# Pooled attention and a spatial gating unit on one core: the engines' order from a list schedule of the kernel's own, normalised rows on ScalarE, first operands early

## The chip, the core and the metric

The kernel runs on one core of one Trainium2 chip. The core has a matrix engine (TensorE, PE in the profile, with its weight loads as PEld), VectorE (DVE), ScalarE (ACT), GpSimd (POOL) and SyncE (SP), which here issues the DMA transfers. Each engine works through its own instructions in order; an instruction that depends on another engine's result waits for a semaphore. SBUF is the on-chip working memory, PSUM the memory of eight banks into which PE writes its products. The metric is the time of one execution in microseconds (us) of device time; the median of the runs is compared.

## The reference

`q`, `k` and `v` have 8 batches, 8 heads, 1152 rows and 64 columns. Attention runs with queries averaged in twos (576 per head); its output, with the heads side by side, goes through a gated unit whose second half is normalised by rows and mixed along the sequence.

```python
q_pool = q.reshape(B, H, S // 2, 2, D).mean(axis=3)
scores = scale * np.matmul(q_pool, k.transpose(0, 1, 3, 2))
attn = np.exp(scores - np.max(scores, axis=-1, keepdims=True))
x = attn / (attn.sum(-1) + 1e-9) @ v             # then heads beside each other: (8, 576, 512)
h = np.maximum(x @ w_in, 0.0)                    # w_in: 512 x 1024
u, v = h[..., :512], h[..., 512:]
v_n = (v - mean(v)) / np.sqrt(var(v) + 1e-6)     # per row
v_s = np.einsum('ts,bsd->btd', w_spatial, v_n) + b_spatial[None, :, None]
out = (u * v_s) @ w_out                          # w_out: 512 x 512
```

## The kernel before

**Pairs.** The 64 heads are worked on as 32 pairs (two heads of one batch; four pairs make a batch). A pair's work:

- `load_kq` and `load_v` (L230, L239) fetch keys, queries and values, 576 KB each.
- `prep` (L286) scales queries and keys by a power of two found from their squares (`square_sum` on ACT, a small matmul in `scales` L117) and splits each number into two 16-bit parts: `head` on ACT (L141), `rest` on DVE (L144), for the keys a subtraction on POOL (L319). Eleven or so DMAs on SP (L310 to L328) copy the parts to where both heads need them.
- `maxima` (L332) has PE form the scores once in one 16-bit product per tile, 27 tiles of 128 x 384 (L355, L346), and DVE take the row maximum of each (L361). `shift` (L369) turns the maxima into two rows of the operand `X`, so that the second pass subtracts them.
- `attention` (L520) forms the scores again, two matmuls a tile (L528, L529), and ACT takes the exponential into `pt` (L534): 18 main tiles of 512 columns. Columns 512 to 576 of both heads are the tail, `ptl` (L542). POOL splits the result into two 16-bit parts, two tiles at a time (L546).
- `values` (L435) multiplies by V (L449, L453, L458), accumulating in the PSUM bank `o`; `tail_values` (L492) does this for the tail (L500 to L502) in the columns of the same bank that the main part leaves free, without the check of accumulation groups. DVE divides by the row sums (L428, L429, L466, L506); `turn_main` (L473) transposes on PE and splits into `xg` (L422, L423).
- `norm_v` (L251) squares V for the scale of a batch, which needs all four pairs of it; `split_v` (L266) scales and splits V (L274, L275 on ACT, L277 on POOL).

**Units.** Two batches (8 pairs) make one of four units (`gated_unit`, L568): the v half of the hidden layer (L605, ReLU on ACT L613, row statistics on DVE L615, L616), a Newton iteration for the inverse root of the variances (L625 to L637, on DVE, all nine row tiles at once), the u half (L669, L679) with `normalise` (L639) once after each of the first nine pieces, the spatial product (L710, L711, L717, L720), a split of the gated result (`split`, L725) and the output product (L753, L773, L795). `normalise` is, per row tile, a subtract and multiply on DVE (L641), a cast to 16 bits on ACT (L646), the remainder on DVE (L647), and for one tile four copies.

The three weight matrices are also split into parts on the chip; `w_in` and `w_out` come as doubles, in pieces of 1024 KB (L187), and are taken apart on DVE and ACT (`from_double`, L150).

**What sets the order.** The program's order comes from the loop at L831: each step of a pair's attention lets the generators for the next pair's maxima, V, preparation and the weights go on at set rates, and `MOE_RATE` steps of a unit. The tile framework then puts the instructions of each engine in an order by its own scheduler and its own estimates, with program order as priority. Ahead of the loop (L819 to L827) stand the first pair's loads, its V squares, its preparation, the next pair's loads, V squares of the rest of the batch, the maxima and V's split.

**PSUM.** Eight banks: `ps_s` 3 (scores), `ps_m` 2 (maxima, small products, transposes), `ps_o` 1 (`o`), `ps_w` 2 (units; maxima too while no unit is under way, L341).

Of the kernel before, what the change touches and what calls it, by code (L numbers as in the profile page):

```python
# [10 lines left out]
F16 = mybir.dt.float16  # L11
BF16 = mybir.dt.bfloat16
F32 = mybir.dt.float32
I32 = mybir.dt.int32
I64 = mybir.dt.int64
U32 = mybir.dt.uint32
AF = mybir.ActivationFunctionType
ALU = mybir.AluOpType
AX = mybir.AxisListType
PSUM = bass.MemoryType.PSUM  # L20
# [8 lines left out]
PEXP = 2.0 ** 6  # L29


@with_exitstack
def attn_sgu_kernel(ctx: ExitStack, tc: tile.TileContext, qT, kT, v, w_in, w_spT, b_sp, w_out, out):
    nc = tc.nc
    P = 128
    B, NHP, _, D, _, S = qT.shape
    NC = kT.shape[4]
# [10 lines left out]
    NT = S2 // P  # L48
# [6 lines left out]
    D1 = D + 1  # L55
    VW = 2 * D + 2

    const = ctx.enter_context(tc.tile_pool(name="const", bufs=1))
    ld = ctx.enter_context(tc.tile_pool(name="ld", bufs=1))
    pp = ctx.enter_context(tc.tile_pool(name="pp", bufs=4))  # L60
    pt_ = ctx.enter_context(tc.tile_pool(name="pt_", bufs=1))
    wk = ctx.enter_context(tc.tile_pool(name="wk", bufs=2))
    mo = ctx.enter_context(tc.tile_pool(name="mo", bufs=1))
    sm = ctx.enter_context(tc.tile_pool(name="sm", bufs=1))
    ps_s = ctx.enter_context(tc.tile_pool(name="ps_s", bufs=3, space=PSUM))
    ps_m = ctx.enter_context(tc.tile_pool(name="ps_m", bufs=2, space=PSUM))
    ps_o = ctx.enter_context(tc.tile_pool(name="ps_o", bufs=1, space=PSUM))
    ps_w = ctx.enter_context(tc.tile_pool(name="ps_w", bufs=2, space=PSUM))


    nc.scalar.preload_act_table_set("natural_log_exp_and_others")
# [59 lines left out]
    def scale_of(sq, name):  # L131
        tot = sm.tile([P, 1], F32, name=name + "t", bufs=2)
        nc.vector.reduce_sum(out=tot, in_=sq, axis=AX.X)
        yield
        return (yield from scales(tot, name))

    def square_sum(acc, src, junk):
        nc.scalar.activation(junk, src, AF.Square, bias=0.0, scale=1.0, accum_out=acc)
# [89 lines left out]
    state = {}  # L228
# [10 lines left out]
    def load_v(i):  # L239
        b, hp = divmod(i, NHP)  # L240
        vt = ld.tile([P, 2, NC, D], F32, name="vt", bufs=2)
        nc.sync.dma_start(
            out=vt.rearrange("p h c d -> p h (c d)"),
            in_=v[b, 2 * hp : 2 * hp + 2].rearrange("h (p c) d -> p h (c d)", c=NC),
        )
        return vt
# [4 lines left out]
    def norm_v(i):  # L251

        b, hp = divmod(i, NHP)
        if hp == 0:
            vsq[b] = sm.tile([P, 2 * NHP], F32, name="vsq", bufs=2)
        vt = load_v(i)
        yield
        yield
        for h in range(2):
            square_sum(vsq[b][:, 2 * hp + h : 2 * hp + h + 1], vt[:, h], vt[:, h])  # L260
            yield
        if hp == NHP - 1:
            vscale[b] = yield from scale_of(vsq.pop(b), "v")
            yield
# [67 lines left out]
    def maxima(i):  # L332
        st = state[i]
        qhl, khh, X = st["qhl"], st["khh"], st["X"]
        W = KEYS // 3
        NB = W // P
        mt = sm.tile([P, NT, 3], F32, name="mt", bufs=2)
        for t in range(NT):
            for n in range(3):

                if units or (t + n) % 2:  # L341
                    pm = ps_m.tile([P, 512], F32, name="pm")
                else:
                    pm = ps_w.tile([P, 512], F32, name="pw")
                if t == 4:
                    nc.tensor.matmul(  # L346
                        pm[:, :W],
                        lhsT=qd[i % 2].rearrange("p h s -> p (h s)"),
                        rhs=st["kn"][:, n * NB : (n + 1) * NB, :],
                        start=True, stop=True,  # L350
                    )
                else:
                    h = 0 if t < 4 else 1
                    c0 = t * P if t < 4 else TAIL + (t - 5) * P
                    nc.tensor.matmul(  # L355
                        pm[:, :W],
                        lhsT=qhl[:, h, c0 : c0 + P],
                        rhs=khh[:, h, n * NB : (n + 1) * NB, :],
                        start=True, stop=True,
                    )  # L360
                nc.vector.reduce_max(out=mt[:, t, n : n + 1], in_=pm[:, :W], axis=AX.X)  # L361
                yield

            if t == 4 and True:
                yield from shift(X, mt, 0, 5)
        yield
        yield from shift(X, mt, 5 if True else 0, NT)
# [40 lines left out]
    xs = {}  # L408
# [83 lines left out]
    def tail_values(i):  # L492

        b, hp = divmod(i, NHP)
        ptl, vp = state[i]["ptl"], vps[i % 2]
        o = state[i]["o"][:, 4 * D1 : 6 * D1].rearrange("p (h d) -> p h d", d=D1)
        for c in range(NC):
            top = ptl.bitcast(BF16)[:, c].rearrange("p h s -> p (h s)")[:, 1::2]
            rst = ptl.bitcast(F16)[:, c].rearrange("p h s -> p (h s)")[:, 0::2]
            nc.tensor.matmul(o, lhsT=top, rhs=vp[:, :, c, D : D + D1], start=False, stop=False, skip_group_check=True)  # L500
            nc.tensor.matmul(o[:, :, 0:D], lhsT=top, rhs=vp[:, :, c, 0:D], start=False, stop=False, skip_group_check=True)
            nc.tensor.matmul(o, lhsT=rst, rhs=vp[:, :, c, D : D + D1], start=False, stop=c == NC - 1, skip_group_check=True)  # L502
        r = inverse(o[:, 0, D : D + 1], "dent")
        for h in range(2):
            rows = slice(h * D, (h + 1) * D)
            nc.vector.tensor_scalar_mul(xt[rows, hp, rows], o[rows, h, 0:D], r[rows])  # L506
# [61 lines left out]
    def gated_unit(un):  # L568
        b0, b1 = 2 * un, 2 * un + 1
# [5 lines left out]
        last = un == NU - 1  # L575
# [20 lines left out]
        vv = mo.tile([P, NT, DH], F32, name="vv")  # L596
        vh = vv.bitcast(F16)
        te = mo.tile([P, 2, DH], F16, name="te")
        mv = mo.tile([P, NT, 2], F32, name="mv")
        for t, (c0, _) in enumerate(tiles):  # L600
            ph = bank()
            n = 0
            for cc in range(NCC):
                for xa, wa in ((xh, wi_h), (xh, wi_l), (xl, wi_h)):
                    nc.tensor.matmul(  # L605
                        ph, lhsT=xa[:, cc, c0 : c0 + P], rhs=wa[:, cc, DH:DF],
                        start=n == 0, stop=n == 3 * NCC - 1,
# [4 lines left out]
            k = 0 if t < 4 else 2 if t == 4 else 1  # L612
# [11 lines left out]
        rs = sm.tile([P, NT], F32, name="rs")  # L624
        nc.vector.tensor_scalar_add(va, mv[:, :, 1], 1e-6)  # L625
        nc.vector.tensor_scalar(
            out=sd.bitcast(I32), in0=va.bitcast(I32), scalar1=1, scalar2=None, op0=ALU.logical_shift_right
        )
        nc.vector.tensor_scalar(
            out=rs.bitcast(I32), in0=sd.bitcast(I32), scalar1=-1.0, scalar2=float(0x5F3759DF), op0=ALU.mult, op1=ALU.add  # L630
        )
        for k in range(4):
# [3 lines left out]
            nc.vector.tensor_scalar(out=sd, in0=sd, scalar1=-0.5 * z, scalar2=1.5 * z, op0=ALU.mult, op1=ALU.add)  # L636
            nc.vector.tensor_mul(rs, rs, sd)  # L637

        def normalise(t):  # L639
            vn = wk.tile([P, DH], F32, name="row")  # L640
            nc.vector.tensor_scalar(  # L641
                out=vn, in0=vv[:, t, :], scalar1=mv[:, t, 0:1], scalar2=rs[:, t : t + 1],
                op0=ALU.subtract, op1=ALU.mult,
            )
            h, l = vh[:, t, 0:DH], vh[:, t, DH : 2 * DH]
            nc.scalar.activation(h, vn, AF.Copy, bias=0.0, scale=1.0)  # L646
            nc.vector.tensor_sub(l, vn, h)  # L647
            if t == 4:

                nc.vector.tensor_copy(out=te[0:TAIL, 0, :], in_=h[0:TAIL])  # L650
                nc.vector.tensor_copy(out=te[TAIL:P, 0, :], in_=l[0:TAIL])
                nc.vector.tensor_copy(out=te[0:TAIL, 1, :], in_=h[TAIL:P])
                nc.vector.tensor_copy(out=te[TAIL:P, 1, :], in_=l[TAIL:P])
# [9 lines left out]
        for fc in range(NFC):  # L663
            for a, z in pieces:
                pu = bank()
                n = 0
                for cc in range(NCC):
                    for xa, wa in ((xh, wi_h), (xl, wi_h), (xh, wi_l)):
                        nc.tensor.matmul(  # L669
                            pu[:, : z - a], lhsT=wa[:, cc, fc * P : (fc + 1) * P], rhs=xa[:, cc, a:z],  # L670
                            start=n == 0, stop=n == 3 * NCC - 1,
# [4 lines left out]
                for e in range(2):  # L676
                    y, w = max(a, e * S), min(z, (e + 1) * S)
# [87 lines left out]
        if not last:  # L765
# [4 lines left out]
            for t in range(NT):  # L770
                py = yield from products(0, t)
                y = wk.tile([P, DM], F32, name="row")
# [3 lines left out]
        else:  # L776
            order = [(e, fc) for fc in range(NFC) for e in range(2)]
# [14 lines left out]
            for t in range(NT):  # L792
                py = yield from products(1, t)
                y = vv[:, t]
# [20 lines left out]
    def drain(gen):  # L815
        while gen is not None:
            gen = step(gen)

    load_kq(0)  # L819
    drain(norm_v(0))  # L820
    drain(prep(0))
    load_kq(1)
    for i in range(1, NHP):
        drain(norm_v(i))
    drain(maxima(0))
    drain(split_v(0))
    drain(prep(1))  # L827
    weights = load_weights()
# [2 lines left out]
    for i in range(NP):  # L831
        if i + 2 < NP:
            load_kq(i + 2)
        run = [
            Pace(maxima(i + 1), MAX_RATE) if i + 1 < NP else None,
            Pace(values_ahead(i), V_RATE),
            Pace(prep(i + 2), PREP_RATE, PREP_AT) if i + 2 < NP else None,
            Pace(weights, W_RATE, W_AT if i == 0 else 0),
        ]
# [17 lines left out]
        turn(last=True)  # L857
    for g in units:
        drain(g)


def _lay(inputs):
# [42 lines left out]
```

## Time and profile before

| | |
|---|---|
| median of 3 runs | 1302.94 us (1302.19 to 1303.21) |
| profiled execution | 1300.77 us, span 1299.0 us |
| mean granted PE clock | 0.986 |
| busy: PE, ACT, DVE, POOL | 1175.9, 974.8, 894.7, 853.8 us |
| PE instructions | 13632 matmuls |
| DMA | 129.04 MB, mean 99 GB/s |
| first exp, first split | 45.4 us, 47.5 us |
| v half of the units begins | 296.6, 601.9, 904.5, 1196.6 us |

How to read it: the span is the time from the first to the last instruction of the profiled execution; the device time also has what lies around it. An engine's busy time counts its own instructions, overlapped ones once. "idle before <- X" is how long an engine stood still ahead of such an instruction, and what ended it. Matmuls overlap in a pipeline, so the duration of a matmul is longer than the distance to the next one.

### The profile page before, as it was taken

To read this page: it belongs to the slowest core of one execution; us is meant where nothing else is said; L and a number is where in the kernel's file an instruction comes from. 1 tells how busy PE (TensorE), PEld (TensorE's weight loads), DVE (VectorE), ACT (ScalarE), POOL (GpSimd) and SP (SyncE) were. 2 spreads that over 40 slices of the span, in tenths; PEclk is the share of its full clock that TensorE was granted. 3 is DMA by queue.
4 is the path that set the end of the run, shared out by engine and by line. 5 is a ranking of instruction groups with operands and counts; after the bars stand their busy time and mean duration, and the time that the engine had idled before them with its cause. 6 is when DMAs were issued, how large, how long until landed. Compare 5 with 4: busy or idle time off the path is not lost. (4 is left out here: it accounts for less than half of the span.)

```text
span 1299.0 us, 33747 instructions
## 1 busy us (share of the span) xinstructions
PE 1175.9 (91%) x13632; PEld 733.6 (56%) x13632; DVE 894.7 (69%) x2060; ACT 974.8 (75%) x1659; POOL 853.8 (66%) x494
## 2 busy tenths in 40 slices
PE   2678888889888999899998999899998999999998
PEld 1355555556555666566654666566565666555454
DVE  4798779786878567855669576865669756751544
ACT  6888988899876977878766877878776886754333
POOL 3688899997655777767664767768675766664000
PEclk9999999899999999999999999999998999999999
DMA  8554553435422333254233342145333211101002
GB/s 273 183 151 110 171 164 97 122 92 152 129 72 66 107 107 107 56 158 144 67 96 89 97 118 75 38 144 143 103 107 89 70 48 47 31 34 42 1 1 73
DMA packets 63421, 129.04 MB, mean 99 GB/s; under 512 B 13792, under 2 KB 21984, under 8 KB 62752
## 3 DMA queue, kind: packets, MB, share of 16 engines
q1 hardware_dynamic: 63264, 126.88, 33.6%
q8 instruction: 107, 1.75, 0.6%
q14 instruction: 50, 0.41, 0.1%
HBM read 83.56 MB, written 9.44 MB: 72 GB/s over the span
## 5 line engine op out<-in xcount | busy, mean ns | idle before, releaser
L546 POOL TENSOR_TENSOR pt<-pt 128x1024 f16<-128x1024 f32 x288 | 573.7, 1998 | 231.5 <-ACT pt L534 228.7
L534 ACT ACTIVATE pt<-pss,lnp,esc 128x512 f32<-128x512 f32 x576 | 440.8, 778 | 147.1 <-PE pss L529 137.9
L361 DVE TENSOR_REDUCE mt<-pm 128x1 f32<-128x384 f32 x730 | 391.8, 551 | 139.2 <-PE pm L355 122.3
L529 PE MATMUL pss<-xq,klo 66*128 66x64 f16 (+1 forms) x1152 | 278.8, 291 | 0.0
L528 PE MATMUL pss<-qhi,khi 128*128 128x64 f16 (+1 forms) x1152 | 272.7, 290 | 6.2 <-ACT pt L534 5.3
L355 PE MATMUL pm<-khi,qhi 128*128 128x384 f16 x652 | 212.7, 330 | 25.0 <-DVE mt L361 22.0
L449 PE MATMUL o<-vp,pt 128*128 128x65 f16 x2304 | 226.2, 195 | 7.4 <-DVE xm L466 6.4
L453 PE MATMUL o<-vp,pt 128*128 128x64 f16 x2304 | 224.9, 194 | 0.0
L449 PEld LDWEIGHTS <-pt 128*128 128x128 bf16 x2304 | 182.2, 99 | 73.1 <-issue 12.8
L453 PEld LDWEIGHTS <-pt 128*128 128x128 bf16 x2304 | 167.3, 99 | 54.8 <-issue 13.6
L458 PE MATMUL o<-vp,pt 128*128 128x65 f16 x2304 | 168.6, 195 | 19.4 <-POOL pt L546 19.1
L458 PEld LDWEIGHTS <-pt 128*128 128x128 f16 x2304 | 111.6, 99 | 25.9 <-POOL pt L546 22.6
L529 PEld LDWEIGHTS <-klo 66*128 66x128 f16 x1152 | 98.3, 99 | 45.4 <-issue 16.3
L528 PEld LDWEIGHTS <-khi 128*128 128x128 f16 x1152 | 102.4, 100 | 34.0 <-issue 16.1
L355 PEld LDWEIGHTS <-qhi 128*128 128x128 f16 x768 | 76.1, 100 | 63.3 <-issue 25.3
L277 POOL TENSOR_TENSOR vp<-vt,vp 128x576 f16<-128x576 f32 x64 | 84.3, 1319 | 39.9 <-ACT vp L275 39.9
L546 POOL TENSOR_TENSOR ptl<-ptl 128x1152 f16<-128x1152 f32 x32 | 69.9, 2185 | 51.7 <-ACT ptl L542 51.7
L542 ACT ACTIVATE ptl<-pss,lnp,esc 128x256 f32<-128x256 f32 (+1 forms) x128 | 75.5, 590 | 22.0 <-PE pss L529 21.8
L319 POOL TENSOR_TENSOR klo<-kt,kn 128x640 f16<-128x640 f32 x64 | 85.0, 1335 | 10.4 <-ACT kn L318 10.4
L605 PE MATMUL pw<-wi_h,xg 128*128 128x512 f16 x240 | 88.9, 378 | 0.0
L361 DVE TENSOR_REDUCE mt<-pw 128x1 f32<-128x384 f32 x134 | 71.9, 544 | 19.7 <-PE pw L355 18.6
L669 PE MATMUL pw<-xg,wi_h 128*128 128x512 f16 (+1 forms) x336 | 81.6, 331 | 0.0
(180 smaller groups left out, 2342.0 us busy)
## 6 DMA issues: line engine op xcount, KB each, us to landing
vt<-in_v_dram SPq DMA_DIRECT2D x64, 576.0 KB
qt<-in_qT_dram SPq DMA_DIRECT2D x32, 576.0 KB
kt<-in_kT_dram SPq DMA_DIRECT2D x32, 576.0 KB
khi<-kn SPq DMA_DIRECT2D x128, 144.0 KB
out_dram<-row SPq DMA_DIRECT2D x24, 256.0 KB
qhi<-xq SPq DMA_DIRECT2D x64, 72.0 KB
klo<-klo SPq DMA_DIRECT2D x32, 144.0 KB
vv<-in_w_in_dram SPq DMA_DIRECT2D x4, 1024.0 KB
```

The source lines that it names most:

```text
L277: nc.gpsimd.tensor_sub(vp[:, h, :, 0:D], vt[:, h], vp[:, h, :, D : 2 * D])
L319: nc.gpsimd.tensor_sub(KL[:, 0, a:z], k0[:, a:z], kn[:, a:z])
L355: nc.tensor.matmul(pm[:, :W], lhsT=qhl[:, h, c0 : c0 + P], rhs=khh[:, h, n * NB : (n + 1) * NB, :], start=True, stop=True,)
L361: nc.vector.reduce_max(out=mt[:, t, n : n + 1], in_=pm[:, :W], axis=AX.X)
L449: nc.tensor.matmul(o[:, t], lhsT=top[:, cols], rhs=vp[:, D : D + D1], start=c == 0 and t == 0, stop=False, skip_group_check=True,)
L453: nc.tensor.matmul(o[:, t, 0:D], lhsT=top[:, cols], rhs=vp[:, 0:D], start=False, stop=False, skip_group_check=True)
L458: nc.tensor.matmul(o[:, t], lhsT=rst[:, cols], rhs=vp[:, D : D + D1], start=False, stop=c == NC - 1, skip_group_check=True,)
L528: nc.tensor.matmul(o, lhsT=khh[:, h, c, :], rhs=qhl[:, h, q], start=True, stop=False)
L529: nc.tensor.matmul(o, lhsT=KL[0:KR, h, c, :], rhs=X[0:KR, h, q], start=False, stop=True)
L534: nc.scalar.activation(pt, ps, AF.Exp, bias=lnp, scale=esc)
L546: nc.gpsimd.tensor_sub(t.bitcast(F16)[:, :, 0::2], t, t.bitcast(BF16)[:, :, 1::2])
L605: nc.tensor.matmul(ph, lhsT=xa[:, cc, c0 : c0 + P], rhs=wa[:, cc, DH:DF], start=n == 0, stop=n == 3 * NCC - 1,)
```

## The change

**Order of instructions.** Every pool is wrapped, so that a class `Order` knows which tile, with which buffer, each instruction reads and writes. At the end of the program, `order.pin(tc)` takes all instructions of the five engines (memsets and a few others left out), finds what each has to follow (`edges`: overlapping accesses, users of a buffer's former tile, for PSUM whole banks between engines, and tiles of one name begin in program order), and gives each a cost (`cost`). It then simulates: at each step the engine that can start first takes, among its instructions that are ready by then, the one that stands first in the program. Each instruction is tied to the one before it on its engine, so that the framework's scheduler has to keep this order. DVE and POOL operations that read two operands from SBUF are simulated as excluding each other; SP's transfers share one wire at 230 bytes per ns.

```diff
+    def cost(self, lane, ins):
...
+        if lane == "PE":
+            n = count(xs[0])
+            t = max(28.5, n / 2.4 + 2.5)
...
+            return t, t + 148
+        if lane == "SP":
+            big = max((count(x) * x.ap[0][1] * self.SIZE[x.dtype] for x in xs), default=0)
+            return 500, 2400 + big / 230
...
+        if lane == "Activation":
+            t = 1.04 * n + (230 if psum else 95)
+        elif lane == "DVE":
+            t = 1.04 * n + 130
+        else:
+            t = (1.75 if any(x.dtype in (F16, BF16) for x in xs[:-1]) else 2.2) * n + 120
+        return t - 80, t
...
+    def pin(self, tc):
...
+            for e, ns in ready.items():
+                if ns:
+                    t = max(free[e], min(due[n] for n in ns))
+                    n = min(n for n in ns if due[n] <= t)
+                    if best is None or t < best[0]:
+                        best = (t, e, n)
...
+            if shared[n]:
+                if e == "DVE":
+                    if t >= held[0]:
+                        t = max(t, held[1] - 130)
+                    dve = t + out
+                else:
+                    t = max(t, dve)
+                    held = (t, t + out)
+            if e == "SP":
+                wire = max(wire, t + own) + (out - 2400)
+                end = wire + 1900
+            else:
+                end = t + out
+            free[e] = t + own
+            if e in last:
+                tc.add_manual_dep(prog[n], last[e], dep, reason="order")
+            last[e] = prog[n].name
...
```

**The tail's bank, the normalised rows, the start.** `tail_values` accumulates in a tile of `ps_m` of its own with ordinary accumulation flags. `normalise` computes `rs * v - mean * rs` in one activation on ACT, with a bias column `nm` that one small DVE operation per unit prepares. Ahead of the loop, the first pair's V squares move behind its preparation and maxima.

```diff
-        o = state[i]["o"][:, 4 * D1 : 6 * D1].rearrange("p (h d) -> p h d", d=D1)
+        ps = ps_m.tile([P, 512], F32, name="pm")
+        o = ps[:, : 2 * D1].rearrange("p (h d) -> p h d", d=D1)
...
+        nm = sm.tile([P, NT], F32, name="nm")
+        nc.vector.scalar_tensor_tensor(out=nm, in0=mv[:, :, 0], scalar=-1.0, in1=rs, op0=ALU.mult, op1=ALU.mult)
...
-            nc.vector.tensor_scalar(
-                out=vn, in0=vv[:, t, :], scalar1=mv[:, t, 0:1], scalar2=rs[:, t : t + 1],
-                op0=ALU.subtract, op1=ALU.mult,
-            )
+            nc.scalar.activation(vn, vv[:, t, :], AF.Identity, bias=nm[:, t : t + 1], scale=rs[:, t : t + 1])
...
     load_kq(0)
-    drain(norm_v(0))
     drain(prep(0))
     load_kq(1)
-    for i in range(1, NHP):
+    drain(maxima(0))
+    for i in range(NHP):
         drain(norm_v(i))
-    drain(maxima(0))
     drain(split_v(0))
...
+    order.pin(tc)
```

More of the change, by code (lines that the diff above doesn't have):

```diff
@@ L56, in attn_sgu_kernel @@
     VW = 2 * D + 2
[L58 to L68, printed above, removed]
+    order = Order()
+    const = order.pool(ctx.enter_context(tc.tile_pool(name="const", bufs=1)), 1)
+    ld = order.pool(ctx.enter_context(tc.tile_pool(name="ld", bufs=1)), 1)
+    pp = order.pool(ctx.enter_context(tc.tile_pool(name="pp", bufs=4)), 4)
+    pt_ = order.pool(ctx.enter_context(tc.tile_pool(name="pt_", bufs=1)), 1)
+    wk = order.pool(ctx.enter_context(tc.tile_pool(name="wk", bufs=2)), 2)
+    mo = order.pool(ctx.enter_context(tc.tile_pool(name="mo", bufs=1)), 1)
+    sm = order.pool(ctx.enter_context(tc.tile_pool(name="sm", bufs=1)), 1)
+    ps_s = order.pool(ctx.enter_context(tc.tile_pool(name="ps_s", bufs=3, space=PSUM)), 3, True)
+    ps_m = order.pool(ctx.enter_context(tc.tile_pool(name="ps_m", bufs=2, space=PSUM)), 2, True)
+    ps_o = order.pool(ctx.enter_context(tc.tile_pool(name="ps_o", bufs=1, space=PSUM)), 1, True)
+    ps_w = order.pool(ctx.enter_context(tc.tile_pool(name="ps_w", bufs=2, space=PSUM)), 2, True)
     nc.scalar.preload_act_table_set("natural_log_exp_and_others")
@@ L499, in tail_values @@
             rst = ptl.bitcast(F16)[:, c].rearrange("p h s -> p (h s)")[:, 0::2]
-            nc.tensor.matmul(o, lhsT=top, rhs=vp[:, :, c, D : D + D1], start=False, stop=False, skip_group_check=True)
-            nc.tensor.matmul(o[:, :, 0:D], lhsT=top, rhs=vp[:, :, c, 0:D], start=False, stop=False, skip_group_check=True)
-            nc.tensor.matmul(o, lhsT=rst, rhs=vp[:, :, c, D : D + D1], start=False, stop=c == NC - 1, skip_group_check=True)
+            nc.tensor.matmul(o, lhsT=top, rhs=vp[:, :, c, D : D + D1], start=c == 0, stop=False)
+            nc.tensor.matmul(o[:, :, 0:D], lhsT=top, rhs=vp[:, :, c, 0:D], start=False, stop=False)
+            nc.tensor.matmul(o, lhsT=rst, rhs=vp[:, :, c, D : D + D1], start=False, stop=c == NC - 1)
         r = inverse(o[:, 0, D : D + 1], "dent")
```

132 lines of the change are left out of this document (added).

## The prediction

> **What bounds the kernel now.** I read the page first (busy shares and the 40 slices), then the busy time in stretches cut where the attention pairs end, then the groups and the waits inside those stretches.
>
> ```profile
> span 1299.0 us, 33747 instructions
> PE 1175.9 (91%) x13632; PEld 733.6 (56%) x13632; DVE 894.7 (69%) x2060; ACT 974.8 (75%) x1659; POOL 853.8 (66%) x494
> PE   2678888889888999899998999899998999999998
> DVE  4798779786878567855669576865669756751544
> POOL 3688899997655777767664767768675766664000
> ```
>
> PE is the busiest engine over the whole, but not everywhere. It starts empty, runs at 8 tenths for seven slices while POOL stands at 8 to 9, and then runs at 9 with three dips in which DVE rises to 8 or 9. In the next view the columns are PE, PEld, DVE, ACT and POOL busy, the granted clock, the DMA share and GB/s. A pair ends with its last split on POOL (L546); 47.5 is the first split.
>
> ```profile
> 0.00:47.50 47.50, 17.55 (x60) 6.17 (x61) 25.10 (x56) 31.45 (x59) 18.69 (x25) 1.00 0.71 233
> 47.50:291.90 244.40, 201.93 (x2797) 137.13 (x2794) 205.02 (x432) 214.91 (x347) 222.16 (x119) 0.97 0.47 136
> 291.90:1192.30 900.40, 853.59 (x10152) 539.77 (x10152) 613.09 (x1452) 691.19 (x1182) 612.93 (x353) 0.99 0.32 91
> 1192.30:1299.00 106.70, 102.80 (x628) 50.49 (x628) 51.47 (x121) 37.27 (x72) 0.00 (x1) 1.00 0.08 26
> 366.20:413.00 46.80, 38.64 (x447) 23.87 (x446) 43.57 (x93) 32.66 (x57) 26.02 (x16) 1.00 0.26 75
> 666.20:715.30 49.10, 41.21 (x447) 24.94 (x446) 44.27 (x93) 32.88 (x57) 25.74 (x15) 0.93 0.25 71
> 715.30:751.80 36.50, 36.05 (x445) 23.27 (x442) 20.06 (x51) 32.05 (x58) 26.45 (x17) 1.00 0.34 95
> 970.00:1016.60 46.60, 41.10 (x447) 24.94 (x446) 42.55 (x93) 31.65 (x53) 26.41 (x15) 0.93 0.22 62
> ```
>
> There are four stages. Start, 47.5 us: latency. Pairs 0 to 7, 244.4 us: POOL 91%, ACT 88%, DVE 84%, PE 83%. Pairs 8 to 31, which share PE with three gated units, 900.4 us: PE 95%. The last unit alone, 106.7 us: PE 96%. In the third stage an ordinary pair (715.3 to 751.8) has PE at 99%; the three pairs that take 46.6 to 49.1 us are those in which a unit normalises its rows, and there DVE is at 90 to 93%.
>
> **The change part by part. Normalised rows.** These are the DVE rows of the first of those pairs, then the same lines in the last unit, where POOL is idle, and ACT's cast from the first.
>
> ```profile
> L361 DVE TENSOR_REDUCE mt<-pm 128x1 f32<-128x384 f32 x29 | 15.4, 550 | 2.0 <-PE pm L355 1.6
> L641 DVE TENSOR_SCALAR row<-vv,mv,rs 128x512 f32<-128x512 f32 x9 | 11.7, 1318 | 0.1
> L647 DVE TENSOR_TENSOR vv<-row,vv 128x512 f16<-128x512 f32 x9 | 9.9, 1108 | 1.1 <-ACT vv L646 1.0
> L634 DVE TENSOR_TENSOR pm<-rs,pm 128x9 f32<-128x9 f32 x4 | 0.7, 167 | 0.0
> ...
> L647 DVE TENSOR_TENSOR vv<-row,vv 128x512 f16<-128x512 f32 x9 | 6.0, 690 | 1.8 <-ACT vv L646 1.7
> L641 DVE TENSOR_SCALAR row<-vv,mv,rs 128x512 f32<-128x512 f32 x9 | 4.5, 542 | 0.1
> ...
> L646 ACT ACTIVATE vv<-row 128x512 f16<-128x512 f32 x9 | 5.5, 627 | 7.3 <-DVE row L641 7.3
> ```
>
> L641 leaves DVE: 11.7 us of 43.6, so 31.9 stay. ACT takes nine activations of the size of L646, 9 x 0.63 = 5.7: 32.7 becomes 38.4, beside PE's 38.6. The new small operation nm is one more of the 0.17 us kind per unit, behind the same chain. So these pairs are then held by ACT and PE together at 38.5 or more; I take 40 us each, 120 for 142.5: **-22**. The far ends: ACT's queue, where each row now waits twice, keeps them at 45 (-7), or they sink to the ordinary 36.5 (-33). In the last unit DVE and ACT are half idle beside PE (51 and 37 of 107): nothing, and if PE's cover were gone, 9 x (0.63 - 0.54) = +0.8.
>
> L641 takes 542 ns with POOL idle and 1318 with POOL at work. The Trainium skill, SBUF — State Buffer, Who interferes with whom, has VectorE and GpSimd share one port pair as an exclusive lock, on which ScalarE never waits; the trace agrees for L641. Its page ScalarE: Activation LUTs, Rules for kernel authors, speaks against the move: multiplies and adds belong on VectorE. By the idle-POOL rows that holds here (542 against 627 ns); by the rows of the three pairs it doesn't (1318). Going by that rule alone the sum would lose the -22 and gain 9 x 0.085 x 4 = 3; that case is a rival below.
>
> **The order.** The list's costs set what the engines will wait for, so I hold them against rows: an exp from PSUM 1.04 x 512 + 230 = 762 ns, a maximum 1.04 x 384 + 130 = 529, a split 1.75 x 1024 + 120 = 1912, a cast 1.04 x 512 + 95 = 627, a 65-column matmul 29.6.
>
> ```profile
> L534 ACT ACTIVATE pt<-pss,lnp,esc 128x512 f32<-128x512 f32 x576 | 440.8, 778 | 147.1 <-PE pss L529 137.9 <-POOL pt L546 4.2 <-PE o L458 3.5
> L546 POOL TENSOR_TENSOR pt<-pt x288: 1888/1898/3112, 47.5 to 1190.4; 128x1024 f16<-128x1024 f32 x144
> 47.50:291.90 244.40, 171.85 (x81) 0.97 0.47 136
> 1199.55 7.77 PE pss L605 x36
> 141.67 0.19 PE L449 MATMUL o<-vp,pt 128*128 128x65 f16 x1
> ...
> 141.88 0.19 PE L453 MATMUL o<-vp,pt 128*128 128x64 f16 x1
> ```
>
> They fit: 778, 550, 1898 (median), 627, and eight value matmuls start within 0.21 us, 30 ns apart. So the fixed order should mostly find its operands ready, and I count it as a gain where engines idle together.
>
> Pairs 0 to 7: the 81 splits took 171.85 us (third row); at the median, and 1.75 x 1152 + 120 = 2.14 for the 8 of 1152 columns, 73 x 1.898 + 8 x 2.14 = 155.7. So 16 us were waits for VectorE, and POOL's floor is 222 - 16 = 206. ACT's is 215, less what is drawn into the idle 16 us of the start. I take ACT at 93%, 232: **-12**. Ends: 220 (-24), and +5 if the three coupled engines keep their gaps and the tail's bank (below) adds to them.
>
> The 21 ordinary pairs of the third stage: (900.4 - 142.5) / 21 = 36.1 us. A 512-column matmul streams in 7.77 / 36 = 0.216 us, 0.42 ns a column. A pair has 18 x 2 x 512 + 36 x 64 + 27 x 384 + 9 x 388 = 34,600 columns outside the values, 14.6 us, and 216 value matmuls, 6.5; an eighth of a unit, 28,800 columns, is 12.1: 33.2 us. Of the 2.9 between, small f32 matmuls take a part that no order removes; I take 0.9 back: **-18**, ends 0 and -2 x 21 = -42. The last unit: PE idles 3.9 us of 106.7: **-2**, ends 0 and -4.
>
> **First operands early.** Starts in the first 47.5 us:
>
> ```profile
> 9.42 0.47 SPq L187 DMA_DIRECT2D vv<-in_w_in_dram  x1
> 11.54 0.67 ACT L138 ACTIVATE vt<-vt 128x576 f32<-128x576 f32 x1
> 12.21 0.76 ACT L141 ACTIVATE xq<-qt,qks 128x576 f16<-128x576 f32 x1
> 15.49 0.69 DVE L156 TENSOR_SCALAR u<-vv 128x1024 int32<-128x1024 int32 x1 [1.17 <-DMA vv<-in_w_in_dram]
> 19.48 0.80 PE L355 MATMUL pw<-khi,qhi 128*128 128x384 f16 x2 [11.49 <-DMA khi<-kn]
> 45.43 1.43 ACT L534 ACTIVATE pt<-pss,lnp,esc 128x512 f32<-128x512 f32 x2
> ```
>
> One square of V (11.54) runs ahead of xq: 0.7 us on the chain to the first matmul at 19.48. Later V squares, V's split and the next pair's preparation stand ahead of the first exp. With the squares behind the maxima in the program and drawn into ACT's 16 idle us, I take the first split 4 us earlier: **-4**. Ends: -9; and +6, because both first weight pieces (1024 KB) depend on nothing, so a list that issues what is ready puts them ahead of the operand copies on SP's one queue, and one took 15.49 - 9.42 = 6.1 us.
>
> **The tail's bank.** tail_values takes a bank of ps_m, which the maxima also use, instead of room in o.
>
> ```profile
> L500 PE MATMUL o<-vp,ptl 128*128 128x130 f16 x288 | 52.7, 221 | 0.0
> L506 DVE TENSOR_SCALAR xt<-o,dent 64x64 f32<-64x64 f32 x64 | 18.0, 282 | 1.3
> DVE dent L428 <- PE o L502: 25.8, 21, 8.4
> ```
>
> Held per pair: 27 matmuls at 130 x 0.42 = 55 ns, 1.5 us; two small DVE operations and two of L506, 0.9; the mean wait 25.8 / 32 = 0.8: 3.2 us. On one bank a maximum takes PE's 0.33 and then DVE's 0.55 instead of 0.55: 3.2 / 0.88 x 0.33 = 1.2 us of DVE a pair. DVE has 16 us to spare in an ordinary pair, so only the eight early and three normalising pairs pay, up to 13; I take **+3**.
>
> Sum: -22 - 12 - 18 - 2 - 4 + 3 = -55. The profiled execution took 1300.8 us (span 1299.0 and 1.8 around it), 2.2 under the median, so 1246 in its terms and **1248** in the median's.
>
> **The rivals.** *The new order is worth nothing by itself* (the present stages are near 95% of some engine already): only the rows' move counts, 1302.9 - 22 = 1281. For it: PE's 99% in the ordinary pair. Against: POOL, ACT and DVE all idle 9 to 16% in the early pairs. *The order packs to the floors*: -33 - 24 - 42 - 4 - 9 with no bank cost is -112; at 90% of that, 1202. Against it: ACT at 38.4 in the normalising pairs, and coupled queues.
>
> *The rows' move is worth nothing*: if the new order already keeps VectorE's rows apart from the splits, L641 would have cost 542 ns there as it does in the last unit, ACT needs 627, and 22 + 3 are missing from the sum: 1248 + 25 = 1273. For it: the two durations; against: a list that goes by readiness has no reason to avoid the splits. (This is the outcome by the rule of ScalarE: Activation LUTs in the Trainium skill.)
>
> *Slower: the tail's bank becomes the wait.* If the list puts the tail's two closing DVE steps behind maxima and row work (the longest wait for them is 8.4 us), the bank is held 8 us a pair; then 8 / 0.88 x 0.33 = 3.0 us of DVE are lost per pair, and PE, whose next maximum is fixed in its queue, stands with it: 32 x 3.0 = 96 less the 3 counted already, 1248 + 93 = 1341. At 5 us, with all 32 pairs paying, it eats the gain (60); from there on the kernel is slower. Against it: DVE's slack in 21 pairs. A milder form, 6 us held, ends at 1317. *The list repeats the present order*, and ACT's longer queue in three pairs eats the row's gain: 1303.
>
> **How the numbers follow.** The forecast 0.45 (1225 to 1270), order worth nothing 0.18, rows' move worth nothing 0.07, packed to the floors 0.12, the bank 0.13, nothing changes 0.05. About 0.2% (2.6 us) is what a measurement can tell from no change. Faster 0.45 + 0.18 + 0.07 + 0.12 = 0.82, same 0.05, slower 0.13. The range 1203 to 1300 leaves out the bank and a part of the packed case.
>
> **What would show it.** Right: the three pairs at 38 to 42 us with DVE under 36 busy and ACT over 36; the early stage near 232 with splits nearer 1.9 us; the first split at 43; ordinary pairs near 35. Wrong: PE waiting for maxima right after tail_values (the bank); the first matmul later than 19.5 behind weight loads (SP's order); the three pairs still over 44 with ACT's wait for rs or the cast in place of DVE; ordinary pairs at 36 (the order gives nothing).

## The result, and the profile after

The changed kernel takes 1255.24 us (median of 4 runs, 1245.8 to 1257.75) against 1302.57 us; the ratio is 0.9623, with a 95% interval of 0.9591 to 0.9656. 1248 was forecast. The profiled execution took 1256.45 us, its span is 1254.6.

The page of the changed kernel, and the stretches that answer to those of before (cut where the attention pairs end; columns PE, PEld, DVE, ACT, POOL busy, granted clock, DMA share, GB/s):

```profile
span 1254.6 us, 33696 instructions
PE 1163.0 (93%) x13632; PEld 729.5 (58%) x13632; DVE 874.4 (70%) x2028; ACT 997.6 (80%) x1695; POOL 844.5 (67%) x494
PE   1778968888999999999999999999999999999998
DVE  5679888877778776785668766775668856751444
...
0.00:45.00 45.00, 15.03 (x47) 5.44 (x48) 30.59 (x53) 24.51 (x44) 11.52 (x19) 1.00 0.77 255
45.00:297.30 252.30, 208.07 (x2793) 140.19 (x2793) 202.28 (x430) 221.30 (x366) 223.07 (x124) 0.95 0.46 129
297.30:1148.50 851.20, 838.32 (x10171) 533.84 (x10171) 593.87 (x1433) 708.26 (x1206) 609.86 (x353) 1.00 0.34 97
1148.50:1254.60 106.10, 101.60 (x625) 50.00 (x622) 47.64 (x113) 43.49 (x81) 0.05 (x1) 0.99 0.08 26
655.30:692.30 37.00, 36.32 (x440) 23.15 (x439) 32.12 (x76) 34.00 (x58) 24.89 (x14) 1.00 0.23 63
692.30:728.10 35.80, 35.80 (x437) 23.14 (x434) 23.85 (x62) 32.45 (x57) 25.84 (x17) 1.00 0.41 114
```

PE's row of digits shows it: the three dips are gone, and the start is still there. The whole gain lies in the stage that pairs 8 to 31 share with the units: 900.4 became 851.2 us. There PE idles 12.9 us (851.20 - 838.32) instead of 46.8, and is busy 15 us less. About 5 of those 15 us are the clock: of the three slow pairs of before, two ran at 0.93 and kept PE busy for 41.2 and 41.1 us, the third ran at 1.00 and needed 38.6 us for as many matmuls; in the changed kernel such a pair has 1.00 (655.3 to 692.3). The Trainium skill, TensorE: Matmul & The Clock Gate, Part 1: The HAM clock gate, has activity release a throttled clock. Two of the three dips of before agree, since they lost both time and clock; the first of them took 46.8 us at full clock. Pairs 0 to 7 became longer.

| term | forecast | profile before to after |
|---|---|---|
| start, to the first split | -4 | 47.5 to 45.0: -2.5 |
| pairs 0 to 7 (with the tail's bank, +3) | -9 | 244.4 to 252.3: +7.9 |
| three normalising pairs | -22 | 142.5 to 110.9: -31.6 |
| the 21 other pairs | -18 | 757.9 to 740.3: -17.6 |
| last unit | -2 | 106.7 to 106.1: -0.6 |
| sum | -55 | -44.4 |

The table is close for the 21 ordinary pairs and for the small terms at the two ends. Whether it has the right causes is another question: the forecast gave the rows' move 22 us and the order, with the new start, 36, and a profile of both at once can't tell.

What PE waited for in the shared stage, before and then after (total us, times, longest):

```profile
PE pm L346 <- DVE xg L423: 17.5, 9, 2.9
PE pm L355 <- DVE mt L361: 17.0, 19, 1.5
...
```

```profile
PE pw L907 <- DVE u L917: 2.5, 6, 0.4
PE pss L724 <- ACT pt L730: 2.5, 3, 1.2
PE pm L550 <- DVE rs L833: 2.0, 3, 0.7
PE pm L541 <- DVE xg L618: 1.9, 1, 1.9
PE pw L550 <- DVE mt L556: 1.7, 1, 1.7
```

Before, 34.5 of the 46.8 us were PE standing in front of a maximum's matmul whose bank VectorE had not freed (`pm`). After, the waits of this kind come to some 4 us. That other work was there to be done meanwhile is not seen in these rows; the run with the list alone, below, shows it.

### The profile page after: what moved, and what is told of

It reads as the page before. It is cut to its first block, busy times and chain, and to the rows that moved or that the text cites. A ratio compares the mean times of both kernels' runs of the same rounds, so it can differ in the third digit from the quotient of the medians.

```text
span 1254.6 us, 33696 instructions
## 1 busy us (share of the span) xinstructions
PE 1163.0 (93%) x13632; PEld 729.5 (58%) x13632; DVE 874.4 (70%) x2028; ACT 997.6 (80%) x1695; POOL 844.5 (67%) x494
## 5 line engine op out<-in xcount | busy, mean ns | idle before, releaser
L742 POOL TENSOR_TENSOR pt<-pt 128x1024 f16<-128x1024 f32 x288 | 565.8, 1972 | 212.4 <-ACT pt L730 201.4
L556 DVE TENSOR_REDUCE mt<-pm 128x1 f32<-128x384 f32 x730 | 386.0, 550 | 115.5 <-PE pm L550 96.5
L724 PE MATMUL pss<-qhi,khi 128*128 128x64 f16 (+1 forms) x1152 | 269.5, 289 | 16.9 <-ACT pt L730 15.3
L725 PE MATMUL pss<-xq,klo 66*128 66x64 f16 (+1 forms) x1152 | 275.6, 290 | 0.0
L550 PE MATMUL pm<-khi,qhi 128*128 128x384 f16 x652 | 207.9, 331 | 17.6 <-DVE mt L556 14.7
L644 PEld LDWEIGHTS <-pt 128*128 128x128 bf16 x2304 | 177.7, 98 | 49.1 <-DVE xm L661 5.4
L648 PEld LDWEIGHTS <-pt 128*128 128x128 bf16 x2304 | 166.3, 99 | 37.0 <-issue 2.0
L653 PEld LDWEIGHTS <-pt 128*128 128x128 f16 x2304 | 116.0, 98 | 16.6 <-POOL pt L742 4.3
L514 POOL TENSOR_TENSOR klo<-kt,kn 128x640 f16<-128x640 f32 x64 | 83.5, 1311 | 12.9 <-ACT kn L513 12.8
```

The lines of the kernel that those rows point to most:

```text
L514: nc.gpsimd.tensor_sub(KL[:, 0, a:z], k0[:, a:z], kn[:, a:z])
L550: nc.tensor.matmul(pm[:, :W], lhsT=qhl[:, h, c0 : c0 + P], rhs=khh[:, h, n * NB : (n + 1) * NB, :], start=True, stop=True,)
L644: nc.tensor.matmul(o[:, t], lhsT=top[:, cols], rhs=vp[:, D : D + D1], start=c == 0 and t == 0, stop=False, skip_group_check=True,)
L648: nc.tensor.matmul(o[:, t, 0:D], lhsT=top[:, cols], rhs=vp[:, 0:D], start=False, stop=False, skip_group_check=True)
L653: nc.tensor.matmul(o[:, t], lhsT=rst[:, cols], rhs=vp[:, D : D + D1], start=False, stop=c == NC - 1, skip_group_check=True,)
L724: nc.tensor.matmul(o, lhsT=khh[:, h, c, :], rhs=qhl[:, h, q], start=True, stop=False)
```

## The experiments

**Which part is the gain?** First the changed kernel without the list: `order.pin(tc)` is taken out, the other edits stay.

```diff
-    order.pin(tc)
```

> The changed kernel without the list: rows on ScalarE, the tail's own bank and the new start stay, the framework's scheduler orders again. Theory A (rows and order are two separate gains): the three normalising pairs fall from 46.6-49.1 us to about 38-40 and the rest of the units' stage stays at 36.1 us a pair, so 1302.6 - 25 = about 1275. Theory B (the rows' move pays only once the list keeps ScalarE's extra work out of the way): the three pairs stay above 44 and the time stays within 10 us of 1302. Theory C (the list itself gives nothing): about 1255.

Measured: 1295.49 us, ratio 0.9954 (0.9932 to 0.9976). The middle pair of the three, and the whole shared stage:

```profile
664.30:709.00 44.70, 39.93 (x430) 23.91 (x429) 35.78 (x82) 35.73 (x60) 24.66 (x14) 0.92 0.22 65
293.20:1187.70 894.50, 851.00 (x10151) 536.90 (x10151) 599.64 (x1430) 709.10 (x1211) 609.32 (x353) 0.99 0.31 92
```

VectorE's load in that pair falls from 44.3 to 35.8 us, under the 36 that the forecast named though by less than its 11.7 us, and it is no longer the bound. The three pairs still take 42.0, 44.7 and 43.4 us, at granted clocks of 1.00, 0.92 and 0.96, and the other 21 average 36.4 instead of 36.1. PE idles 43.5 us in the stage (894.50 - 851.00), nearly the 46.8 of before, so VectorE's load had not been the reason alone, and a lower clock isn't the reason alone either, since the first pair had all of it. The three smaller edits together are worth 0.5%. This lies between Theory A and B, nearer B.

Then the reverse, the kernel before with the list and nothing else:

> The kernel before with nothing but the list: rows on VectorE, tail in o, former start. Theory A2 (the list is nearly the whole gain, the three other edits are worth a few us under it): 1255 to 1266, the three normalising pairs about 40 us as with the rows alone put back, others about 35. Rival (the edits need each other: the single reverts looked cheap because the other edits covered them): above 1272.

Measured: 1257.40 us, 0.9644 (0.9582 to 0.9706). Its shared stage and the same two pairs as above:

```profile
302.50:1152.80 850.30, 837.83 (x10143) 533.75 (x10141) 603.99 (x1448) 684.54 (x1172) 618.34 (x352) 1.00 0.33 96
654.80:697.80 43.00, 40.98 (x487) 25.95 (x485) 35.20 (x86) 31.24 (x55) 26.44 (x14) 1.00 0.19 54
697.80:732.10 34.30, 33.62 (x413) 21.66 (x411) 27.78 (x61) 27.77 (x51) 26.58 (x17) 1.00 0.29 84
```

This is the reading that decides the case. With the rows on VectorE the normalising pair is 43.0 us long, six more than in the changed kernel; but its neighbour is shorter, and the stage is 850.3 against 851.2. In the 43.0 us PE is 41.0 busy and runs 487 matmuls, not 440: work of the neighbours has moved in (99 matmuls of the unit's u half instead of 78, 86 of the scores' second pass instead of 72). When PE is full, a pair's length says where PE's work was put and not what it cost.

**The small edits one by one, under the list.** The rows back on VectorE:

```diff
-            nc.scalar.activation(vn, vv[:, t, :], AF.Identity, bias=nm[:, t : t + 1], scale=rs[:, t : t + 1])
+            nc.vector.tensor_scalar(
+                out=vn, in0=vv[:, t, :], scalar1=mv[:, t, 0:1], scalar2=rs[:, t : t + 1],
+                op0=ALU.subtract, op1=ALU.mult,
+            )
```

> The changed kernel with the subtract-and-multiply of the rows back on VectorE, list kept. Theory A: the three pairs return to about 45 us, the rest stays: 1255 + 25 = about 1280. Theory B': a list that knows the lock between VectorE and GpSimd spreads the rows by itself, so that the move is worth little under it: 1255 to 1263, the three pairs under 40.

Measured: 1260.40 us, 0.9665 (0.9621 to 0.9708), an interval that overlaps the changed kernel's; the shared stage is 853.2 us, the three pairs 39.7 to 40.1. Theory B' stands in its time and, at the edge, in its pairs, but not in its reason: a row on VectorE beside the attention pairs still takes 0.99 us on average (27 rows), against 1.21 in before and 0.54 alone. The list does not keep rows and splits apart; the move is worth little because PE is full either way, 840.5 of 853.2 us.

The tail's products back in `o`:

```diff
-        ps = ps_m.tile([P, 512], F32, name="pm")
-        o = ps[:, : 2 * D1].rearrange("p (h d) -> p h d", d=D1)
+        o = state[i]["o"][:, 4 * D1 : 6 * D1].rearrange("p (h d) -> p h d", d=D1)
```

> The changed kernel with the tail's products back in the free columns of o, list kept. If the bank that the tail takes from the maxima costs, as I put it (+3 and up to +13 in the early pairs): 1242 to 1252, and the 244 to 252 us stage of pairs 0 to 7 shrinks. If the shared bank o ties the tail to the main values and their division in a fixed order: slower, 1258 to 1275.

Measured: 1257.81 us, 0.9664 (0.9642 to 0.9687); the early stage is 258.0 us instead of 252.3. The bank that the maxima lose costs nothing that can be measured; the direction is the other one, within the uncertainty.

The former order ahead of the loop:

```diff
     load_kq(0)
+    drain(norm_v(0))
     drain(prep(0))
     load_kq(1)
-    drain(maxima(0))
-    for i in range(NHP):
+    for i in range(1, NHP):
         drain(norm_v(i))
+    drain(maxima(0))
```

> The changed kernel with the former program order ahead of the loop (V's squares first), list kept. Theory: the list draws ready work forward anyway, so the start hardly moves: first split within 3 us of 45.0, time 1253 to 1260. Rival (the early pairs suffer because V's squares now come late): the first split goes back to 47.5 or later, but pair 1 falls from 40.2 us to about 30 and the time to 1245 to 1250.

Measured: 1255.79 us, 0.9643 (0.9615 to 0.9671). The expected time, but neither picture: the first split comes at 56.4 us, 11 later than in the changed kernel, and the early stage then takes 241.9 us, 10 less. Pair 7 ends at 298.3 us against 297.3.

**Why the early stage did not shrink.** Pair 7 ends at 291.9 us in before, 293.2 without the list (although its first split comes at 34.2), 297.3 in the changed kernel. A first suspect is the conversion of the weights, which runs on VectorE and ScalarE during pairs 0 to 7. In this run it stops after its first two steps, and four VectorE operations and one of ScalarE on each piece are left out:

```diff
         nc.scalar.activation(dst, t1, AF.Copy, bias=1.0, scale=2.0 ** -20)
         yield
+        return
```

> The changed kernel in which the doubles' conversion ends after its first VectorE and ScalarE step (the low word, the exponent and the sign are left out, four VectorE operations and one of ScalarE on each of the six pieces of 128 x 1024). Theory E (the early stage is long because the weights' conversion shares VectorE and ScalarE with pairs 0 to 7): its 252 us fall to 225 or less, pair 1 from 40 to about 30, time about 1230. Rival (the conversion fits into gaps, and the early stage is held by the order of the products' bank and SP's queue): 245 or more, time above 1247.

Measured: 1238.8 us in its one run. The early stage and the time of its 81 splits, and that time in the changed kernel:

```profile
46.30:279.40 233.10, 208.06 (x2850) 139.56 (x2847) 169.06 (x427) 221.16 (x376) 210.71 (x124) 0.94 0.52 147
46.30:279.40 233.10, 156.62 (x81) 0.94 0.52 147
```

```profile
45.00:297.30 252.30, 165.09 (x81) 0.95 0.46 129
```

252.3 became 233.1, between the two expectations. The splits take 156.6 us, which is nearly the floor of 155.7 that the forecast worked out; with the conversion they take 165.1, and 171.9 in before. So 7 of the 16 us in which splits waited are gone in the changed kernel (5 of them in the run without the list too, where the splits take 167.1), and the conversion's operations make nearly all the rest. The Trainium skill, SBUF — State Buffer, Who interferes with whom, names an exclusive lock between VectorE and GpSimd. The rows agree. What is left is ScalarE: 221 of 233 us, 95%.

The pairs tell more. Here are pairs 1 and 4 of before, then the same two of the changed kernel, and the VectorE operation that splits queries (`rest`), before and after (shortest, median and longest time in ns), with PE's wait in pair 4:

```profile
79.60:107.50 27.90, 22.78 (x315) 15.32 (x316) 22.36 (x50) 25.32 (x42) 25.51 (x15) 0.95 0.57 163
167.80:197.30 29.50, 24.30 (x353) 17.10 (x350) 23.40 (x52) 26.16 (x42) 28.78 (x18) 1.00 0.51 152
75.70:115.90 40.20, 30.55 (x375) 20.38 (x372) 33.83 (x75) 31.98 (x53) 34.88 (x20) 0.96 0.43 107
168.20:202.50 34.30, 22.57 (x282) 15.18 (x282) 30.98 (x50) 22.70 (x36) 25.50 (x16) 0.85 0.31 93
...
L144 DVE SCALAR_TENSOR_TENSOR qhi<-qt,qks,xq x32: 808/1180/2840, 13.0 to 1101.5; 128x576 f16<-128x576 f32 x32
L339 DVE SCALAR_TENSOR_TENSOR qhi<-qt,qks,xq x32: 795/818/12116, 9.4 to 1061.1; 128x576 f16<-128x576 f32 x32
187.82 0.80 PE L550 MATMUL pm<-khi,qhi 128*128 128x384 f16 x2 [9.69 <-DVE mt L556]
```

Pair 1 is 12 us longer, but it also holds more work of every engine, and pairs 2 and 3 are 8 us shorter. Pair 4 is a loss: it does less and takes longer. One `rest`, usually 0.8 us, starts at 175.0 us and ends at 187.1. GpSimd begins seven operations one right behind the other in this time, and `rest` ends 0.6 us after the last of them. Behind it stand a maximum's reduction, PE for 9.7 us and ScalarE for 7.9 us, and from 182 to 186 us the granted clock is 0.50. In two other runs the longest `rest` ends 0.6 us behind GpSimd's last operation as well, after 12.1 us with the rows put back and after 9.8 us with the tail in `o`. In the run below that holds the weights' loads back behind the copies, the longest `rest` takes 2.5 us and pair 4 28.7 us. The list's model lets VectorE wait for one GpSimd operation and then makes the next wait for VectorE; the trace shows otherwise. This is not the whole of the early stage's length, which is 252 us in that run too.

**The list's estimate of the transfers.** In the changed kernel's start, weight loads of 1024 KB and other loads stand between the copies of the first pair's operands on SP's queue:

```profile
12.53 0.46 SPq L516 DMA_DIRECT2D khi<-kn  x1
13.04 0.58 SPq L382 DMA_DIRECT2D vv<-in_w_in_dram  x1
...
18.64 0.59 SPq L517 DMA_DIRECT2D khi<-kn  x1
21.57 0.46 SPq L519 DMA_DIRECT2D khi<-kn  x1
22.14 0.54 SPq L520 DMA_DIRECT2D khi<-kn  x1
...
28.51 0.48 PE L550 MATMUL pw<-khi,qhi 128*128 128x384 f16 x1 [20.56 <-DMA khi<-kn]
```

The first maximum's matmul starts at 28.5 us; in before it was 19.5. I first took the list's estimate of the wire for the cause, since single loads land faster:

```diff
-            return 500, 2400 + big / 230
+            return 500, 2400 + big / 390
```

> The changed kernel with one number of the list's costs changed: SP's transfers at 390 bytes per ns instead of 230 (the first loads of 576 KB landed 1.5 us apart in the trace of before). Theory D (the list expects the operand copies late, so it puts 1024 KB weight pieces and other loads between them on SP's queue; the first matmul came at 28.5 us instead of 19.5, and the early stage starts in an order made for late data): first matmul at 18 to 24 us, pairs 0 to 7 done by 285 instead of 297, time 1240 to 1248. Rival (the early stage is held by ScalarE, GpSimd and VectorE anyway): pairs 0 to 7 done at 293 to 300 whatever the start, 1252 to 1258.

Measured: 1286.40 us, 0.9871 (0.9819 to 0.9924), 31 us slower than the changed kernel, against both expectations. The early stage is 264.8 us and the shared one 876.9. The waits of ScalarE's squares for keys and for values, at 390 and then at 230:

```profile
ACT klo L333 <- DMA kt<-in_kT_dram: 29.6, 16, 4.0
ACT vt L333 <- DMA vt<-in_v_dram: 28.2, 12, 4.5
```

```profile
ACT klo L333 <- DMA kt<-in_kT_dram: 2.1, 3, 1.4
ACT vt L333 <- DMA vt<-in_v_dram: 7.7, 6, 2.2
```

An instruction that the list places too early blocks its engine until its data is there, and everything behind it. The estimate is not only a forecast but a margin, and fixing an order is not enough by itself. With closer costs of ScalarE and of markers on SP besides:

```diff
-            return 500, 2400 + big / 230
+            if ins.opcode == "TilePoolBoundary":
+                return 0, 2400
+            return 500, 2400 + big / 390
...
-            t = 1.04 * n + (230 if psum else 95)
+            t = 0.835 * n + (350 if psum else 205)
+            if len(ins.outs) > 1:
+                t += 190
```

> As the run with 390 bytes per ns, and also: ScalarE at 0.835 n + 205 (SBUF) or + 350 (PSUM) ns with 190 for a sum read out, and nothing on SP for markers that are no transfers. Theory D: a further step the same way, first matmul at 14 to 20 us, 1230 to 1243. Rival as there: 1250 to 1258.

Measured: 1280.19 us, 0.9825 (0.9776 to 0.9875): Theory D fails again. And with more margin:

```diff
-            return 500, 2400 + big / 230
+            return 500, 2400 + big / 170
```

> The changed kernel with SP's transfers at 170 bytes per ns in the list's costs instead of 230. Theory G (the list's estimate of the transfers works as a margin: 390 made engines wait for data that came later than listed; more margin costs only a little): 1250 to 1262, fewer waits for loads than in the changed kernel. Rival (the time has its best at the true effective rate, and a list that expects data late holds work back): 1265 or more, like 390.

Measured: 1262.67 us, 0.9692 (0.9648 to 0.9736). The shared stage is 848.9 us, as good as at 230; the loss is in the start, with the first split at 50.2 us, and in the early stage, 255.5. The time lies just past the 1262 of Theory G and under its rival's 1265; the waits shown above fall to 2.6 us in all, as the theory said. The error is cheap on one side and dear on the other.

**The start by a rule instead of an estimate.** The first weight loads may not pass the first pair's copies:

```diff
+        sp = [n for n, i in enumerate(prog) if names[i.engine] == "SP" and i.opcode == "DMACopy"]
+        for n in sp:
+            a = [self.access(x) for x in prog[n].outs if hasattr(x, "bass_ap")]
+            if a and a[0] and (a[0][0][0], a[0][0][1]) == ("vv", 0) or a and a[0] and a[0][0][0] == "b_bc":
+                before[n].update(m for m in sp[2:14] if m != n)
```

> The changed kernel with one rule more for the list: the first weight loads (1024 KB each) and b_spatial's load may not stand on SP's queue ahead of the first pair's twelve operand copies. Theory F (9 us of the early stage's length come from these loads between the copies): first matmul at about 18 us instead of 28.5, pairs 0 to 7 done by 285 to 290 instead of 297, time 1243 to 1250. Rival (whatever the start gives is taken back, because the conversion of the weights then falls into pairs 0 to 7 instead of the wait ahead of them): first matmul early, pairs 0 to 7 still done at 294 or later, time 1252 to 1260.

Measured: 1246.93 us (1245.69 to 1248.04), 0.9573 (0.9522 to 0.9625).

```profile
18.17 0.59 SPq L525 DMA_DIRECT2D khi<-kn  x1
...
20.24 0.50 SPq L387 DMA_DIRECT2D vv<-in_w_in_dram  x1
...
23.06 0.48 PE L555 MATMUL pw<-khi,qhi 128*128 128x384 f16 x1 [15.03 <-DMA khi<-kn]
...
41.70:294.10 252.40, 213.31 (x2831) 141.03 (x2830) 203.21 (x439) 229.62 (x381) 230.90 (x124) 0.93 0.48 140
294.10:1137.90 843.80, 833.83 (x10130) 531.07 (x10128) 582.58 (x1424) 703.00 (x1199) 609.82 (x352) 1.00 0.33 97
```

The first maximum comes 5.4 us earlier, the first split 3.3 us, and the early stage keeps its 252 us, so pair 7 ends at 294.1. The shared stage is 7.4 us shorter, for which the edit gives no reason; a new list is made from the changed start on, and it falls out otherwise. The time is the one of Theory F, the end of pair 7 the one of its rival. The median is the lowest of all kernels here that do the whole work. Its interval overlaps the changed kernel's, one run of which took 1245.8 us, so that it beats it is likely and not shown.

The markers' cost set to nothing as well, and in another run ScalarE's closer costs instead (both as in the diff above, at 230 bytes per ns):

> As the run with the weights behind the copies, and eleven markers at the list's start, which are no transfers, cost SP nothing (they put all loads 5.5 us later in the list than they are). Theory F: another 1 to 4 us less, since pair 0 is ordered for data that comes earlier. Rival (a lower estimate of the loads is dangerous, as with 390 bytes per ns): 2 to 15 us more.

> The run with the weights behind the copies (1246.9), and the list's cost of ScalarE fitted to the rows: 0.835 n + 205 ns from SBUF, + 350 from PSUM, and 190 for a sum read out. If closer costs of one engine make a better order (at 390 bytes per ns the closer costs of ScalarE and the markers together went from 1286 to 1280): 1238 to 1244. Rival (the costs of ScalarE are close enough, and the order is as good as the program order allows it): 1245 to 1250.

Measured: 1248.83 us, 0.9586 (0.9542 to 0.9631), and 1251.21 us, 0.9612 (0.9593 to 0.9630). Neither makes it faster, which is what both rivals said (the second lies just past its rival's 1250); the early stage stays at 254.9 and 258.2 us. Its length is between 242 and 258 us in every run at 170 or 230 bytes per ns that has the list and the whole conversion, whatever the edit. It is longer, by and large, where the granted clock in it is lower (0.96 at 241.9, 0.95 at 252.3, 0.90 at 258.0 us); which of the two leads to the other is not shown.

## Why the prediction was right or wrong

**The time and its sign** were right. Two of the five terms were not, and one cause was wrong. That the sum came so near is in part luck: the three normalising pairs gave 10 us more than forecast, and pairs 0 to 7 took 17 us more.

- *Normalised rows, -22.* The size in the three pairs was forecast too small, and the cause was wrong. Nearly the whole gain is the order's: the list alone brings 0.9644. Without it the three smaller edits together bring 6 us (1295.5 against 1301.2), and under it putting the rows back costs 5 us within the uncertainty. The step that failed is "these pairs are then held by ACT and PE together at 38.5 or more; I take 40": with VectorE's load gone the pairs still took 42 to 45, since most of the lost time came from the order in which PE met VectorE's results: with the list they took 37, with or without the move the stage took 850 to 853. The rival "the rows' move is worth nothing" was right on the worth of the move and not on its reason, since rows on VectorE take 0.99 us under the list and not 0.54; its 1273 was wrong, because the order brought what the rows did not.
- *ScalarE's price, 9 x 0.63.* Mis-sized: an activation with a column for scale and one for bias takes 0.81 us (median of the 36 below), not 0.63 as the cast does. The forecast "ACT over 36" was still missed on the low side, 34.0, since only 7 of the nine rows fall into the pair.

```profile
L841 ACT ACTIVATE row<-vv,nm,rs x36: 802/813/847, 380.1 to 1194.8; 128x512 f32<-128x512 f32 x36
```

- *The 21 ordinary pairs, -18.* Measured -17.6, and PE waits behind it gone, as said. But the split between these and the three normalising pairs is arbitrary while PE is full: with the list alone the 21 take 34.4 us and the three 43. The stage as a whole was forecast at -40 and gave -49.
- *Pairs 0 to 7, -12.* Wrong in sign: +7.9, past even its upper end of +5. The step that failed is "I take ACT at 93%": ScalarE was at 221 / 252 = 88%, as before. Splits were freed from VectorE (171.9 to 165.1 us, most of it without the list too), but POOL then idled more, 29 us instead of 22. For this stage the forecast counted what VectorE costs GpSimd and put the other direction at nothing: one VectorE operation held up by GpSimd made PE stand still for 9.7 us and ScalarE for 7.9. The weights' conversion accounts for 19 us of the stage, by one run. Why the order made the loaded engines mesh no better in the rest of the stage isn't settled: that SP's start order is the whole cause is ruled out (first split from 41.7 to 56.7 us, pair 7 between 294.1 and 302.5 us in all runs with the list at 230 and the whole conversion); that tiles of one name must begin in program order, which ties maxima, scales, transposes and the tail through `pm`, is argued from the code and wasn't tried.
- *Start, -4.* -2.5, with both of its ends at work: the chain to `xq` is shorter (8.6 instead of 12.2 us), and the loads ahead of the copies cost the 6 us and more that stood as the upper end (28.5 against 19.5 us for the first maximum).
- *The tail's bank, +3,* and with it the slower rival: not seen in the time. PE waits 2.6 us in all to get the bank for the tail, the weight loads of maxima wait 4.7 us in all, in 16 places, for the VectorE step that frees it, and the kernel with `o` is not faster.

```profile
PE pm L696 <- DVE mt L556: 2.6, 3, 1.0
```

## What to carry to other kernels

When one engine is full for a whole stage, judge a stage by its end, not by the stretch that looks worst: taking load off VectorE in three slow pairs moved PE's work to other pairs and hardly moved the end, while an order in which PE nearly always found something ready removed 34 us of idle time. A fixed order needs costs that err late: transfers estimated too slow cost 7 us, too fast 31. Where early transfers must not be passed, a rule on the queue brought the first maximum 5.4 us forward here, and neither 170 nor 390 bytes per ns gave a faster kernel than 230.

## What the runs showed that I had not expected

- ScalarE's activation of 128 x 512 from SBUF takes 0.81 us with columns for scale and bias, 0.63 as a plain cast.
- A VectorE operation with two operands in SBUF, 0.8 us by itself, took 12.1 us while GpSimd ran seven operations without a gap, and ended 0.6 us after the last of them.
- Loads of 576 KB land 1.5 us apart when they follow each other from a quiet start, yet a list that counts on this rate, 390 bytes per ns, makes ScalarE wait 58 us for keys and values over the kernel, against 10 at 230.
